# The second MLP product as seven half-size block products instead of eight, with the sums on VectorE

## The chip, the cores and the metric

The kernel runs on one core of a Trainium2 chip. The metric is the device time of one execution in microseconds (us). A core has TensorE (PE, matrix products, with its weight loads listed apart as PEld), VectorE (DVE), ScalarE (ACT), GpSimd (POOL) and SyncE (SP), which mainly issues DMAs. Each engine runs its own queue of instructions in order; semaphores tie the queues together. Products land in PSUM, and DVE or ACT must take them out of it ("drain" it) before a bank can be used again.

## The reference

Attention with a local window of 96 keys and 8 global keys, then a mixing step and an MLP with layer norm, cut to what matters:

```python
def _attn_ref(q, k, v, n_global, n_local):        # (4, 8, 768, 64)
    scores = scale * np.matmul(q, k.transpose(0, 1, 3, 2))
    ...
    scores = np.where(keep, scores + bias, -1e9)
    a = np.exp(scores - max); a = a / sum(a)
    return np.matmul(a, v)
def _moe_ref(x, w_ch1, w_ch2):                     # x (4, 768, 512)
    mixed = np.real(np.fft.fft(np.fft.fft(x, axis=1), axis=2))
    u = x + mixed
    un = (u - mean(u)) / np.sqrt(var(u) + 1e-6)
    ch = np.maximum(un @ w_ch1, 0.0) @ w_ch2       # 512 -> 2048 -> 512
    return u + ch
```

The change concerns the last product, `relu(...) @ w_ch2`, and the sum behind it.

## The kernel before

**Tiling.** The four batches have 768 rows each. The MLP works in chunks of 256 rows, three to a batch, so 12 chunks, c = 0 to 11. A chunk has two row tiles t of 128.

**Per batch.** Attention: `trans` turns q and k of a head pair into qkT (pt, L449), `score` makes the scores (sc, L493), ACT takes their exponentials (er, L516), DVE multiplies them with a mask (ex, L531), and `av` makes the output (pav, L612 and L623), which DVE normalizes into x (L643). `bounce` writes x to DRAM and reads it back in another order as xr. `fold_s` and `fold_d` (L686 to L755, called f1 to f4, g1 and g2 here) are sums and differences on DVE that shrink the Fourier step; `y_unit` (py, L775 and L778) makes its first product, `mirror` reverses parts on POOL, `u_unit` (pu, L856) makes the second, and DVE adds xr to give u (L875). A scaled copy un is transposed by `nt_unit` (ptu, L920) to unT.

**Per chunk.** `ph_unit`, eight per chunk, makes two blocks of 128 of the 2048 hidden columns (ph, L948, 8 matmuls of 256 columns each); ACT (L954) or DVE (L955) takes the relu into hT, [128, 16 blocks, 256 rows] fp16. `pg_unit`, two row tiles by four parts, multiplies hT with w2 (pg, L971, 16 matmuls of 512 columns for a row tile, in one PSUM bank); then one DVE instruction (L982) adds pg, scaled by 1/std, to u, into an output buffer ob, which SP writes to DRAM (L987).

**Order.** A planner in the kernel (`Plan`) writes every queue out when the program is built. It holds four streams of TensorE work, in order of preference: MIX (mixing step), ATT (attention), PH (first product) and PG (second product). From MIX and ATT it may pick among the next ten units, from PH and PG only the first. It gives every DVE, ACT, POOL and SP step an assumed duration, keeps a clock for each engine, and picks the unit that it thinks can start first. So second products fill TensorE where nothing else is ready. The order is then fixed: an engine waits at the head of its queue.

**Buffers.** NBUF gives the number of rotating buffers of each name: hT 3, qs (staging of q and k) 3, u 4, x 1, xr 1, ob 2. PSUM has two banks for pg. In batch 0 hT's buffers also take q and k of three head pairs, and the fourth goes through qs. Weights are loaded by POOL (`wload`, L1057 and L1060), w1 early and w2 in four parts after the last v cast of batch 1.

Of the kernel before, what the change touches and what calls it, by code (L numbers as in the profile page):

```python
# [14 lines left out]
P = 128  # L15
# [144 lines left out]
def dve(n):  # L160
    return 0.15 + n / 960.0


def dve2(n):
    return 0.16 + n / 1920.0
# [7 lines left out]
def kernel(  # L173
# [82 lines left out]
    def bank(tag, name, dtype=FP32):  # L256
# [4 lines left out]
        if "late" not in early:  # L261
# [4 lines left out]

    NBUF = {"hT": 3, "vs": 2, "qk": 2, "qs": 3, "qkT": 4, "er": 2, "eg": 1, "x": 1, "xr": 1, "zy": 1, "eA": 1,
            "ww": 1, "rev0": 1, "u": 4, "un": 2, "unT": 2, "ob": 2}

# [17 lines left out]
    w1 = kon.tile([P, ND, 4 * Dm], FP16, tag="w1", name="w1")  # L287
    w2 = kon.tile([P, NJ, Dm], FP16, tag="w2", name="w2")
    mhalf = kon.tile([P, 2], FP32, tag="mhalf", name="mhalf")
# [16 lines left out]
    def load(b, hp, which):  # L306
# [11 lines left out]
        elif which == "v":  # L318
# [6 lines left out]
            pl.later([("SP", 0.9, run)], free(vtag, vi) + gate, 0.0, [("ld", "v", n)], lat=1.6, dma=2.45)  # L325
        elif b == 0 and hp < 3:
            cell = {}

            def run(cell=cell):
                cell[0] = buf("hT", hp, [P, 2, NS, 2 * Dh], FP32, 2)  # L330
                for w, src in enumerate((q, k)):
                    qk_dma(cell[0][:, w], src, b, h0)
            pl.later([("SP", 0.9, run)], free("hT", hp), 0.0, [("ld", "qk", n, w) for w in range(2)], lat=1.6, dma=2.4)
            for w in range(2):
                cast_qk(b, hp, w, lambda w=w, cell=cell: cell[0][:, w], ("hT", hp))
        else:
            for w, src in enumerate((q, k)):
                cell = {}
                i = 2 * (n - 3) + w

                def run(cell=cell, src=src, i=i):
                    cell[0] = buf("qs", i, [P, NS, 2 * Dh], FP32, 1)
                    qk_dma(cell[0], src, b, h0)
                pl.later([("SP", 0.45, run)], free("qs", i) + gate, 0.0, [("ld", "qk", n, w)], lat=1.6, dma=1.2)
                cast_qk(b, hp, w, lambda cell=cell: cell[0], ("qs", i))
# [251 lines left out]
    def av(b, part, jp):  # L597
# [8 lines left out]
        def run(start, ring):  # L606
# [31 lines left out]
            def norm():  # L638
                if b not in X:
                    X[b] = buf("x", b, [P, NS, Dm], FP16, 4 if b else 5)  # L640
                rc = wk.tile([P, 2, nh, 1], FP32, tag="rc", name=f"rc_{b}_{first}_{jp}", bufs=2)
                V.reciprocal(rc, pv[:, :, :, 64:65])
                VT(X[b][:, 2 * jp:2 * jp + 2, first * Dh:(first + nh) * Dh].rearrange("p j (h d) -> p j h d", d=Dh),  # L643
                   pv[:, :, :, 0:Dh], rc.to_broadcast([P, 2, nh, Dh]), op=ALU.mult)
            pl.later([("DVE", 0.18 + dve(128 * nh), norm)], free("x", b), e, [("x", b, hp, jp) for hp in part], CD(b),
                     ring=ring, rank=RA(b))
# [5 lines left out]
    def bounce(b):  # L652

        on, eng = ("ACT", nc.scalar) if b else ("SP", nc.sync)
        for half in range(2):
            def wr(half=half):
# [4 lines left out]
                for t in range(2):  # L661
                    eng.dma_start(rows[t], X[b][64 * t:64 * t + 64, :, c])
            pl.later([(on, 1.2, wr)], [("x", b, hp, jp) for hp in (2 * half, 2 * half + 1) for jp in range(NP)] + [("xw", b, 0)][:half], 0.0,
                     [("xw", b, half)], [("free", "x", b)], lat=1.6, dma=2.5)

        def rd():
            XR[b] = buf("xr", b, [P, NS, Dm], FP16, 3)
            rows = XD[b].rearrange("(m r) d -> m r d", r=6)
            eng.dma_start(XR[b], rows)
        pl.later([(on, 0.5, rd)], [("xw", b, 0), ("xw", b, 1)] + free("xr", b), 0.0, [("xr", b)], lat=1.6, dma=4.0)  # L670

    def fold_s(b):
# [3 lines left out]
        for n, (c0, cw) in enumerate(parts):  # L676
# [25 lines left out]
            def f4(c0=c0, cw=cw, cell=cell):  # L702
# [6 lines left out]
                     + (free("zy", 2 * b) if n == 0 else []), 0.0,  # L709
                     [("f1", b, n)], [("free", "x", b)] * (2 if len(hps) == HP else 1))  # L710
            pl.later([("DVE", 2 * dve2(2 * cw), f2)], [("f1", b, n)] + free("ww", IW(b, n)), 0.0, [("f2", b, n)])
# [133 lines left out]
    def u_unit(b, pr):  # L845
# [4 lines left out]
        def run(start, ring):  # L850
# [20 lines left out]
            def add():  # L871
                u = UT[c] = buf("u", HP + c, [P, 2, Dm], FP32, 2)
                sm = MV[c] = wk.tile([P, 2, 4], FP32, tag="sm", name=f"sm_{c}", bufs=6)
                for a, rr in enumerate((r0, r1)):
# [5 lines left out]
            pl.later([("DVE", 2 * dve(512) + 0.15, add)], [("xr", b)] + free("u", HP + c), e, [("u", c)],  # L880
                     [("free", "xr", b)] + CD(b), ring=ring)
            cell = {}
# [55 lines left out]
    def ph_unit(c, jp):  # L938
        needs = [("unT", c), ("w1", jp // 2)] + (free("hT", 3 + c) if jp == 0 else []) + [("CD",)]

        def run(start, ring):
            if jp == 0:
                HT[c] = buf("hT", 3 + c, [P, NJ, CH], FP16, 2)
            ph = bank("ph", f"ph_{c}_{jp}")
# [12 lines left out]
        PH.append((needs, ("ph",), run))  # L957

    GP = {}

    def pg_unit(c, t, part):
        b, pr = divmod(c, NP)
        rs = PAIRS[pr][t]
        needs = [("h", c, 2 * part), ("h", c, 2 * part + 1), ("w2", part)]

        def run(start, ring):
            if part == 0:
                GP[0] = bank("pg", f"pg_{c}_{t}")
            pg = GP[0]
            for jb in range(4 * part, 4 * part + 4):  # L970
                nc.tensor.matmul(pg, HT[c][:, jb, t * P:(t + 1) * P], w2[:, jb, :],  # L971
                                 start=(jb == 0), stop=(jb == NJ - 1))
            e = pl.pe(mm_us(512, 4), start)
            if part < 3:
                return
            pl.used(("free", "hT", 3 + c), e)
            i = 2 * c + t
            cell = {}

            def add():  # L980
                cell[0] = buf("ob", i, [P, Dm], FP32, 1)
                V.scalar_tensor_tensor(cell[0], pg, MV[c][:, t, 3:4], UT[c][:, t, :],  # L982
                                       op0=ALU.mult, op1=ALU.add)
            pl.later([("DVE", dve(512), add)], [("rstd", c)] + free("ob", i), e, [("ob", i)], [("free", "u", HP + c)], ring="pg", rank=0)

            def st():
                nc.sync.dma_start(out[b].rearrange("(m r) d -> m r d", r=6)[:, rs, :], cell[0])  # L987
            pl.later([("SP", 0.45, st)], [("ob", i)], 0.0, [], [("free", "ob", i)], lat=1.6, dma=0.7)
        PG.append((needs, ("pg",) if part == 0 else None, run))

# [4 lines left out]
    with tc.manual_schedule():  # L995
# [58 lines left out]
        def wload(i):  # L1054
# [4 lines left out]
            else:  # L1059
                nc.gpsimd.dma_start(w2[:, 4 * a:4 * a + 4, :],  # L1060
                                    moe_w_ch2[a * 512:(a + 1) * 512, :].rearrange("(c p) f -> p c f", p=P))
        for i in range(8):
            needs = [("ld", "qk", 3, 1)] if i == 0 else [("v", 1, HP - 1)] if i == 4 else [("wl", i - 1)]
            pl.later([("POOL", 0.85, lambda i=i: wload(i))], needs, 0.0,
                     [("w1" if i < 4 else "w2", i % 4)], lat=2.0, dma=2.6, rank=1 if i < 4 else 2,
                     then=lambda t, i=i: pl.tok.__setitem__(("wl", i), pl.t["POOL"]))
        for b in range(B):
            if b:
# [52 lines left out]
        for c in range(NP * B):  # L1121
            for jp in range(NJ // 2):
                ph_unit(c, jp)
            for t in range(2):
                for part in range(4):
                    pg_unit(c, t, part)
        pl.run([(MIX, True), (ATT, True), (PH, False), (PG, False)])
# [35 lines left out]
```

The softmax here doesn't subtract the row's maximum and nothing guards it: scores larger than these inputs give would overflow.

## Time and profile before

| what | value |
|---|---|
| timed runs | 290.87, 291.68 and 292.29 us; median 291.68 |
| profiled execution | span 288.0 us from first to last instruction; its own total is not listed apart |
| median less span | 3.7 us |
| PE, PEld busy | 256.0 (89%), 172.7 (60%) |
| DVE, ACT, POOL busy | 183.3 (64%), 142.5 (49%), 59.2 (21%) |
| first product ph, 768 matmuls | 94.0 us busy |
| second product pg, 384 matmuls | 91.1 us busy |
| drains of pg, 24 on DVE | 18.0 us busy |
| moved by DMA | 37.04 MB, 129 GB/s mean |

Busy time of an engine is the union of its instructions; the mean duration of a group can be longer than the distance between two of its instructions, since they overlap. The page cuts the span into 40 slices of 7.2 us and gives the busy share of each engine in tenths. In the group lists each row has the source line, engine, operation, output and inputs, count, then busy time and mean duration, then the idle time in front of it and what ended it.

### The profile page before, as it was taken

What the parts mean: (1) busy time and instruction counts of PE and PEld (TensorE: products, weight loads), DVE (VectorE), ACT (ScalarE), POOL (GpSimd) and SP (SyncE); (2) the same over time, 40 slices, a digit from 0 to 9 for tenths busy, and PEclk for the clock granted to TensorE, in tenths of its full rate; (3) what the DMA queues carried; (4) which work ended last, traced back from release to release, by engine and by line L of the source; (5) the groups of instructions that cost most, each with busy time, mean ns of one, the idle gap of its engine ahead of it and who ended that gap; (6) DMA issues with size and microseconds to landing.
All of it is one profiled execution on the core that took longest, in us unless ns stands there. A gap on an engine that the chain in (4) does not pass through costs nothing.

```text
span 288.0 us, 5961 instructions
## 1 busy us (share of the span) xinstructions
PE 256.0 (89%) x2436; PEld 172.7 (60%) x2436; DVE 183.3 (64%) x380; ACT 142.5 (49%) x224; POOL 59.2 (21%) x124
## 2 busy tenths in 40 slices
PE   1788338799886999989999999999999999999994
PEld 1335226687654646677688466875775767777441
DVE  3516997877744997887679968675897582211121
ACT  2577803888744315567754235778142255544100
POOL 1373006237211111641101113301000411100000
PEclk9999859999997999999999999999999999999999
DMA  7999979799999999913302711100144010010111
GB/s 215 289 293 184 191 237 179 162 216 180 186 220 158 241 253 278 225 52 105 109 2 68 245 73 39 40 0 2 45 103 148 36 73 2 36 39 0 73 75 73
DMA packets 62378, 37.04 MB, mean 129 GB/s; under 512 B 20368, under 2 KB 58512, under 8 KB 62352
## 3 DMA queue, kind: packets, MB, share of 16 engines
q1 hardware_dynamic: 52896, 27.76, 40.0%
q0 software_dynamic: 4224, 4.19, 9.3%
q10 hardware_dynamic: 5232, 4.72, 5.7%
q8 instruction: 19, 0.31, 0.5%
q14 instruction: 7, 0.06, 0.1%
HBM read 31.42 MB, written 9.44 MB: 142 GB/s over the span
## 4 chain that ended last, share of the span: by engine, by line
PE 76%; DMA 9%; DVE 7%; SPq 3%; ACT 3%; issue 1%; DVEq 0%; ACTq 0%
PE pg L971 28%; PE ph L948 26%; DMA qs<-in_k_dram 6%; PE sc L493 3%; PE pav L623 3%; PE pu L856 3%; PE pt L449 3%; SPq L349 3%; PE py L775 2%; DMA qs<-in_q_dram 2%; PE ptu L920 2%; PE py L778 2%; DVE u L875 1%; PE pav L612 1%; DVE x L643 1%
## 5 line engine op out<-in xcount | busy, mean ns | idle before, releaser
L948 PE MATMUL ph<-unT,w 128*128 128x256 f16 x768 | 94.0, 273 | 2.4 <-DVE u L875 2.1
L971 PE MATMUL pg<-w,hT 128*128 128x512 f16 x384 | 91.1, 382 | 0.0
L948 PEld LDWEIGHTS <-w 128*128 128x128 f16 x768 | 71.8, 98 | 18.3 <-issue 7.8
L971 PEld LDWEIGHTS <-hT 128*128 128x128 f16 x384 | 36.4, 98 | 37.1 <-issue 2.0
L954 ACT ACTIVATE hT<-ph 128x512 f16<-128x512 f32 x56 | 33.4, 597 | 39.1 <-PE ph L948 39.0
L982 DVE SCALAR_TENSOR_TENSOR ob<-pg,sm,u 128x512 f32<-128x512 f32 x24 | 18.0, 750 | 41.7 <-PE pg L971 37.5
L516 ACT ACTIVATE er<-sc 128x992 f16<-128x992 f32 (+2 forms) x36 | 32.8, 923 | 19.1 <-PE sc L493 16.9
L955 DVE TENSOR_SCALAR hT<-ph 128x512 f16<-128x512 f32 x40 | 27.5, 689 | 22.3 <-PE ph L948 22.2
L531 DVE TENSOR_TENSOR ex<-er,mk 128x992 f16<-128x992 f16 (+2 forms) x36 | 23.3, 653 | 5.0 <-ACT er L516 4.9
L360 ACT ACTIVATE qk<-qs 128x768 f16<-128x768 f32 x21 | 17.3, 839 | 18.2 <-DMA qs<-in_k_dram 7.3
L824 POOL COPY ww<-zy 128x512 f16<-128x512 f16 x16 | 10.0, 654 | 55.4 <-PE py L775 33.8
L791 ACT ACTIVATE zy<-py 128x512 f16<-128x512 f32 (+1 forms) x12 | 9.6, 810 | 21.6 <-PE py L778 13.3
L623 PE MATMUL pav<-v,ex 128*128 128x65 f16 x352 | 16.7, 196 | 3.8 <-ACT er L516 3.0
L455 DVE COPY qkT<-pt 128x1536 f16<-128x1536 f16 x15 | 14.3, 951 | 8.8 <-PE pt L449 8.8
L775 PE MATMUL py<-t,ww 128*128 128x256 f16 x48 | 11.9, 303 | 8.9 <-DVE ww L740 8.9
L623 PEld LDWEIGHTS <-ex 128*128 128x128 f16 x352 | 15.6, 99 | 6.6 <-issue 4.7
L493 PE MATMUL sc<-qkT 64*128 64x256 f16 (+1 forms) x192 | 17.6, 265 | 1.0 <-DVE qkT L455 1.0
L643 DVE TENSOR_TENSOR x<-pav,rc 128x512 f16<-128x512 f32 (+1 forms) x27 | 17.1, 632 | 0.9
L875 DVE SCALAR_TENSOR_TENSOR u<-pu,xr 128x512 f32<-128x512 f32 x24 | 15.6, 687 | 2.3 <-PE pu L856 2.0
L420 POOL CAST v<-vs 128x768 f16<-128x768 f32 x12 | 10.6, 885 | 27.2 <-DMA vs<-in_v_dram 27.0
L464 POOL COPY kG<-qkT 64x8 f16<-64x8 f16 x32 | 7.8, 244 | 38.6 <-DVE qkT L455 37.7
L449 PE MATMUL pt<-ident,qk 128*128 128x128 f16 x192 | 14.0, 225 | 1.9 <-ACT er L516 0.9
(93 smaller groups left out, 286.3 us busy)
## 6 DMA issues: line engine op xcount, KB each, us to landing
out_dram<-ob SPq DMA_DIRECT2D x24, 256.0 KB, 2.0
qs<-in_q_dram SPq DMA_DIRECT2D x13, 384.0 KB, 5.4
qs<-in_k_dram SPq DMA_DIRECT2D x13, 384.0 KB, 6.5
vs<-in_v_dram SPq DMA_DIRECT2D x24, 192.0 KB, 6.7
w<-in_moe_w_ch_dram POOLq DMA_DIRECT2D x8, 512.0 KB, 10.0
xd<-x ACTq DMA_DIRECT2D x12, 192.0 KB, 3.8
xr<-xd ACTq DMA_DIRECT2D x3, 768.0 KB, 4.3
u<-in_v_dram SPq DMA_DIRECT2D x4, 384.0 KB, 6.3
```

The source lines that it names most:

```text
L449: nc.tensor.transpose(o[:, j % 2], src[:, w, j].rearrange("p h d -> p (h d)"), idn)
L493: nc.tensor.matmul(pa[:, s, c0:c0 + cw], TT[n][lo:lo + 64, 1, i * P:(i + 1) * P], TT[n][lo:lo + 64, 0, i * P:i * P + cw], start=(b > 0), s ...
L516: A(mine(), cut(pa), AF.Exp, 0.0, 0.125)
L531: VT(o, mine(), m, op=ALU.mult)
L623: nc.tensor.matmul(po[:, jj, hh * 65:(hh + 1) * 65], lhsT, v16[b % 2][:, i, h, 0:65], start=(jp == 0 and a == 0), stop=(a == len(ops) - 1) ...
L643: VT(X[b][:, 2 * jp:2 * jp + 2, first * Dh:(first + nh) * Dh].rearrange("p j (h d) -> p j h d", d=Dh), pv[:, :, :, 0:Dh], rc.to_broadcast( ...
L875: V.scalar_tensor_tensor(u[:, a].rearrange("p (n r) -> p n r", r=4), pu[:, a].rearrange("p (r n) -> p n r", r=4), 1.0, XR[b][:, rr].rearra ...
L948: nc.tensor.matmul(ph[:, a * CH:(a + 1) * CH], w1[:, d, jb * P:(jb + 1) * P], UNT[c][:, d, :], start=(d == 0), stop=(d == ND - 1))
L954: pl.later([("ACT", act(512), lambda: A(dst, ph, AF.Relu)), ("DVE", dve(512), lambda: V.tensor_scalar_max(dst, ph, 0.0))], [], e, [("h", c ...
L955: ("DVE", dve(512), lambda: V.tensor_scalar_max(dst, ph, 0.0))],
L971: nc.tensor.matmul(pg, HT[c][:, jb, t * P:(t + 1) * P], w2[:, jb, :], start=(jb == 0), stop=(jb == NJ - 1))
L982: V.scalar_tensor_tensor(cell[0], pg, MV[c][:, t, 3:4], UT[c][:, t, :], op0=ALU.mult, op1=ALU.add)
```

## The change

hT's 16 hidden blocks are the inner dimension of the product. Split it in halves: h is then a 2x2 block matrix (row tile t by half of the hidden columns), w2 one too (half of its rows by half of its 512 columns). Eight block products of 8 matmuls of 256 columns would give the output; Winograd's form of Strassen's method needs seven and some sums. After the change:

- `w2_sums`: eight fp16 DVE sums of 1024 elements, once, give the weight blocks w2t (three of them) and one in place.
- `s_sums`: four DVE sums of 1024 elements a chunk: S1 and S2 and S4 in buffers sx, S3 in place in hT.
- `pg_units`: seven products in five units (p1; p45; p6; p32; p7) in two PSUM banks, A and D. Bank A is drained after p1, after p6 and after p7, bank D after p45 and after p32. Each drain scales by 1/std and accumulates into u in place; p7's goes to both column halves. Products that several outputs share are added on their drained copies or stay in the bank for the next product.
- The output is written from u; ob goes. hT has 2 buffers instead of 3, qs 2 instead of 3; x and xr share one. Batch 0's third and fourth q and k are staged in the space that w2 takes afterwards, and w2's parts are loaded in the order 0, 2, 1, 3.

```diff
-    NBUF = {"hT": 3, "vs": 2, "qk": 2, "qs": 3, "qkT": 4, "er": 2, "eg": 1, "x": 1, "xr": 1, "zy": 1, "eA": 1,
-            "ww": 1, "rev0": 1, "u": 4, "un": 2, "unT": 2, "ob": 2}
+    NBUF = {"hT": 2, "vs": 2, "qk": 2, "qs": 2, "qkT": 4, "er": 2, "eg": 1, "x": 1, "zy": 1, "eA": 1,
+            "ww": 1, "rev0": 1, "u": 4, "un": 2, "unT": 2, "w2": 1, "sx": 4}
...
-            XR[b] = buf("xr", b, [P, NS, Dm], FP16, 3)
+            XR[b] = buf("x", 2 * b + 1, [P, NS, Dm], FP16, 3)
...
+    def w2_sums(i):
+        def run():
...
+            VT(w2t[:, 1, k0, :], b22, b12, op=ALU.subtract)
+            VT(b12, b12, b11, op=ALU.subtract)
+            VT(w2t[:, 0, k0, :], b22, b12, op=ALU.subtract)
+            VT(w2t[:, 2, k0, :], b21, w2t[:, 0, k0, :], op=ALU.subtract)
+        pl.later([("DVE", 4 * dve2(1024), run)], [("w2", i), ("w2", 2 + i)], 0.0, [("w2t", i)], rank=1)
...
+        def s1():
+            VT(new(0), block(1, 0), block(1, 1), op=ALU.add)
+        def s3():
+            VT(block(1, 0), block(0, 0), block(1, 0), op=ALU.subtract)
+        def s2():
+            VT(new(1), SX[c, 0], block(0, 0), op=ALU.subtract)
+        def s4():
+            VT(new(2), block(0, 1), SX[c, 1], op=ALU.subtract)
...
-            for jb in range(4 * part, 4 * part + 4):
-                nc.tensor.matmul(pg, HT[c][:, jb, t * P:(t + 1) * P], w2[:, jb, :],
-                                 start=(jb == 0), stop=(jb == NJ - 1))
...
+        def prod(o, lhs, rhs, first, last=True):
+            for j in range(NK):
+                nc.tensor.matmul(o, lhs(j), rhs(j), start=(first and j == 0), stop=(j == NK - 1), skip_group_check=True)
...
+        def p1(start, ring):
+            A_ = GP[c, "A"] = bank("pg", f"pgA_{c}")
+            prod(A_[:, 0:HC], a(0, 0), bw(0, 0), True)
...
+            pl.later([("DVE", dve(HC), lambda: stt(u(0)[:, 0:HC], A_[:, 0:HC], 0, u(0)[:, 0:HC]))],
...
+        def p45(start, ring):
+            D_ = GP[c, "D"] = bank("pg", f"pgD_{c}")
+            prod(D_[:, 0:HC], a(1, 1), tw(2), True)
+            prod(D_[:, HC:Dm], sx(0), bw(0, 1), True)
...
+        def p6(start, ring):
+            prod(A_[:, 0:HC], sx(1), tw(0), False)
...
+        def p32(start, ring):
+            prod(D_[:, HC:Dm], sx(2), bw(1, 1), False)
+            prod(D_[:, 0:HC], a(0, 1), bw(1, 0), True)
...
+        def p7(start, ring):
+            prod(A_[:, 0:HC], a(1, 0), tw(1), False)
...
+                stt(o, A_[:, 0:HC].unsqueeze(1).to_broadcast([P, 2, HC]), 1, o)
...
+        PG.append((h0 + ws, ("pg",), p1))
+        PG.append((h1 + [("s", c, 1)], ("pg",), p45))
+        PG.append(([("s", c, 2), ("ra", c, 0)], None, p6))
+        PG.append(([("s", c, 4), ("rd", c, 0)], None, p32))
+        PG.append(([("s", c, 3), ("ra", c, 1)], None, p7))
```

## The prediction

> **What bounds the kernel now.** I read the page's parts 1 and 2 first, then the busy time by stretches, the groups by line, and the timeline where attention of one batch ends. Engine rows, then the fortieths of the span:
>
> ```profile
> PE 256.0 (89%) x2436; PEld 172.7 (60%) x2436; DVE 183.3 (64%) x380; ACT 142.5 (49%) x224; POOL 59.2 (21%) x124
> ...
> PE   1788338799886999989999999999999999999994
> ...
> DVE  3516997877744997887679968675897582211121
> ...
> PEclk9999859999997999999999999999999999999999
> DMA  7999979799999999913302711100144010010111
> ```
>
> TensorE is nearly full from the fourteenth slice on; before that it starves while the DMA engines are at 9. VectorE (DVE) is the second engine, and its slack lies in the last quarter, not in the middle. The stretches (length, then PE, PEld, DVE, ACT, POOL busy, clock, DMA share, GB/s):
>
> ```profile
> 60.00:89.00 29.00, 25.22 (x256) 18.19 (x254) 18.32 (x28) 20.44 (x32) 8.92 (x18) 1.00 1.16 198
> 89.00:113.00 24.00, 23.27 (x201) 13.57 (x199) 20.20 (x38) 6.96 (x9) 4.01 (x8) 0.93 1.04 242
> 113.00:169.00 56.00, 54.85 (x559) 38.57 (x558) 46.44 (x86) 31.48 (x50) 13.23 (x24) 1.00 0.45 117
> 169.00:221.00 52.00, 52.00 (x533) 37.41 (x531) 40.29 (x80) 27.86 (x46) 7.91 (x19) 1.00 0.17 56
> 236.00:288.00 52.00, 48.04 (x323) 31.01 (x321) 9.93 (x18) 16.58 (x31) 1.77 (x4) 0.99 0.12 46
> ```
>
> From 89 to 221 DVE is 77 to 84% busy already. The groups concerned (by form), and the fold stage of batch 2 in the timeline:
>
> ```profile
> L948 PE MATMUL ph<-unT,w 128*128 128x256 f16 x768 | 94.0, 273 | 2.4 <-DVE u L875 2.1 <-ACT unT L928 0.2
> L971 PE MATMUL pg<-w,hT 128*128 128x512 f16 x384 | 91.1, 382 | 0.0
> L971 PEld LDWEIGHTS <-hT 128*128 128x128 f16 x384 | 36.4, 98 | 37.1 <-issue 2.0
> L982 DVE SCALAR_TENSOR_TENSOR ob<-pg,sm,u 128x512 f32<-128x512 f32 x24 | 18.0, 750 | 41.7 <-PE pg L971 37.5 <-DMA out_dram<-ob 2.9 <-issue 1.2
> ...
> L692 DVE TENSOR_TENSOR ww<-eA 128x1024 f16<-128x1024 f16 x3 | 2.1, 693 | 0.2
> ```
>
> ```profile
> 156.92 7.07 PE L971 MATMUL pg<-w,hT 128*128 128x512 f16 x32
> 159.84 0.74 DVE L982 SCALAR_TENSOR_TENSOR ob<-pg,sm,u 128x512 f32<-128x512 f32 x1
> 165.98 0.27 PE L775 MATMUL py<-t,ww 128*128 128x256 f16 x1
> 166.85 2.75 PE L971 MATMUL pg<-w,hT 128*128 128x512 f16 x12
> ```
>
> This is what matters: the second product is TensorE's filler. While DVE folds (about 155 to 167) and while y becomes the next unT (py at 165.98, first ph at 180.52 in the chain), pg runs, and 16 of its matmuls ask DVE for one drain. L971 never waited (0.0).
>
> **What the Trainium skill says.** "VectorE: DVE Perf Modes", section "The perf-mode tier table (the rule you actually need)": a two-tensor 16-bit op within SBUF goes at most at 2x, one with a PSUM operand at 1x. The trace agrees: 1024 fp16 elements take 693 ns, 512 fp32 out of PSUM 750. "GPSIMD Engine Reference", section "1. Specifications": GpSimd's SBUF interfaces are shared with DVE instructions that have two SBUF inputs. The trace fits: the 1536-element subtraction L687 took 1.58 us beside a POOL cast at 155.9, about 0.95 otherwise. "TensorE: Matmul & The Clock Gate", section "Why this matters for your kernels": idle gaps over some 3 us cost clock. Here, after the pause at 85.6 to 88.6, the clock of 88 to 92 was 0.61.
>
> **The change, part by part.** Durations are of the profiled execution, whose span is 288.0. Its own total isn't listed apart; I take the median run's 291.68 and call the 3.7 us beyond the span constant.
>
> *TensorE, removed.* 80 pg matmuls run in 17.28 us in the chain, 0.216 each; 16 ph matmuls of 256 columns in 1.75, 0.109 each. Before 384 x 0.216 = 82.9; after 12 chunks x 7 products x 8 = 672 x 0.109 = 73.5. **Gain 9.4**; the work left is 256.0 - 9.4 = 246.6. The 288 further weight loads cost nothing: one takes 98 ns, under the 109 of its matmul, as in L948.
>
> *DVE, added.* Back to back the 1024-element fp16 ops start 0.61 apart (99.80, 100.41, 101.01): 48 sums on h are 29.3 and 8 on the weights 4.9. A chunk's drains become three of 512 and two of 256 instead of two of 512. A 512 drain holds DVE 0.65 (159.84 to 160.50). A 256 one isn't shown: its bounds are 0.20 (pitch of a 256-element fp16 op) and 0.65; I take 0.38, since in L643 256 elements less save 0.27. So 12 x (3 x 0.65 + 2 x 0.38) = 32.5 against 15.6, +16.9. **Sum +51**, DVE about 234. That fits the span; where it falls doesn't.
>
> *Early, 60 to 89.* hT falls from three buffers to two, so in TensorE's queue 16 ph units stand ahead of the first product where 24 stood, and the third chunk waits for all seven products of the first. The products need all of w2 and the weight sums. w2 is still issued on POOL's queue behind the fourth v cast (66.2 in the trace) and landed 10 to 14.6 us after issue, so by about 83; eight sums end near 88. Out of 60 to 89 go 8 ph units (7.0), eight pg matmuls (1.7) and the scores of the last head pair (1.0); one product (0.9) comes in. TensorE is busy 25.2 - 8.8 = 16.4 of 28: idle 11.6, 3.8 before. About 2 us of low clock follow (0.61 above). qs falls from three buffers to two: q and k loads on SP's queue wait for a cast sooner and the v loads behind them as well; v is reordered ahead of q there, so I charge nothing. The w2 loads, the fp16 cast and this wait are hidden by the same starvation.
>
> *Fold stages.* I walked both queues for batch 1, zero at the last av matmul. DVE: norm to 1.1, f1 to f3 with a drain and a relu to 6.4, f4 and the second chunk's drains to 10.2, g1 to 12.1, its last drains 13.4. TensorE ends that chunk at 11.8, but the third chunk's first product reuses the bank, and starts at 13.5: stall 1.7. Then S2, a drain, S3 and g2 (to 17.5) stand on DVE ahead of the drain of the D bank and S4 (19.1); P3 needs both while TensorE stopped at 17.0: stall 2.2. py, though ready at 12.1, is queued behind P3 and starts at 20.9. From there to the first ph (about 32.6) only P7 (0.9) is left as filler, where before 36 matmuls (7.8 us) lay: idle some 3. In all **7** for batch 1; batch 2 by the same walk **8** (1.0 + 1.5 + 2.6, then 3); batch 3, whose order keeps two products after py, **6**.
>
> *Elsewhere.* Between folds DVE has about 30 us of work against 37 of TensorE: 1 us each for the first product behind the last drain, 2 in all. At the end, the last chunk's D drain stands behind S2, S3, S4 on DVE: stall 1.5; drain and output are the 4.0 of before.
>
> *At nothing:* out written from u instead of ob (the same 24 writes on SP; u comes free a landing, 2 us, later, but has four buffers and is next needed after the fold); x and xr sharing one buffer (the read waits for f1, done while the xd writes land, 3.8); batch 0's fourth q and k staged in w2's space (w2 is not loaded before 66).
>
> *Sum.* Work 246.6; idle before 60: 60 - 37.6 = 22.4, kept; 11.6 + 2 early; 7 + 8 + 6 folds; 2; 5.5 end: 311.1. Matmul ends, 0.16 us each, are in the 256 as busy and overlap some 20 stalls: minus 3. Span 308.1, **time 311.8**.
>
> **The rivals.**
> - *Faster: TensorE stays covered.* For it: L971 waited 0.0, and DVE has a third of the span free. Then 9.4 is gained and about 3 lost early: 291.7 - 9.4 + 3 = 285. It decides once all added idle stays under 9.4, that is w2 summed by 80 and each fold's stalls under 2 us. Against it: the folds' DVE queue leaves no room, and the filler is finished before the latency it covered. 0.05; a draw at 291 another 0.05.
> - *Half the stalls.* Short drains at the lower bound and ACT taking relus let DVE run ahead: folds 10 instead of 21, early 3 less: 298 to 300. 0.22.
> - *DVE the outright bound.* The sums run at one element a cycle, for strides or for POOL's sharing. By L643's slope 256 elements cost 0.27, so 1024 would cost 0.5 more: 56 x 0.5 = 28 on DVE, of which I put half on the path: 326. For it: the 1.58 us. Against: L531's masked 960-element ops, strided too, take 685 ns. 0.12.
> - My forecast 0.56.
>
> That the change computes other than it says I find no room for: 672 matmuls stand in the queue.
>
> **How the numbers follow.** The likeliest gives 311.8. The range, 297 to 325, takes the half-stall case, the unknown drains, and most of the outright bound; it leaves out the draw and the gain. About 0.5% is what a measurement of this kernel tells from no change: faster 0.05, same 0.05, slower 0.90.
>
> **What would show it.** The product line with 672 matmuls near 73 to 82 us busy; its waits now on DVE, 15 us or more; DVE 225 to 245 busy; TensorE's slices near 76 to 88 at about half; three dips after the first 100 us, each before the first ph of a batch; relus of ACT idling longer. I am wrong if TensorE stays at 9 throughout, if w2t's sums end before 80, or if the sums average over 1 us.

## The result, and the profile after

The changed kernel takes **314.37 us** (median of four runs, 312.40 to 316.37), the kernel before 291.27 beside it: ratio **1.081, 95% interval 1.073 to 1.090**; the medians are 23.1 us apart. The profiled execution has a span of 311.0 us, 23.0 more than the 288.0 before. Some executions of one and the same kernel ran at a lower granted clock and took longer; the ratios leave them out, and the profiles of e5_load and e1_qs3 are of such executions.

First the page, engine rows and fortieths of the span (a slice is 7.8 us now):

```profile
PE 255.5 (82%) x2724; PEld 204.1 (66%) x2724; DVE 232.3 (75%) x468; ACT 143.7 (46%) x228; POOL 59.6 (19%) x124
...
PE   2798077993199987779999976789999987899994
...
DVE  3438979899648997588779996677788998762553
...
PEclk9799679997569998999999997999999999999998
```

TensorE's busy time has not fallen (255.5 against 256.0), VectorE's rose by 49.0. TensorE's row of nines has three dips after the first 100 us (slices 15 to 18, 24 to 27 and 33 to 35), each before a batch's first `ph`; in the row before, only slice 18 read under 9 there, with an 8. The clock row has new digits under 9 as well.

The stretches are cut at the same events as the forecast's stages: first `ph` of batch 0, then for each batch its last `av` matmul and its first `ph`. Columns: length, then PE, PEld, DVE, ACT, POOL busy, granted clock, DMA share, GB/s.

```profile
52.40:102.10 49.70, 38.03 (x413) 29.64 (x410) 38.46 (x62) 25.14 (x40) 18.56 (x29) 0.83 1.09 200
102.10:136.70 34.60, 27.47 (x273) 23.00 (x272) 27.93 (x57) 12.33 (x16) 5.87 (x13) 0.95 0.63 162
136.70:171.50 34.80, 34.80 (x409) 27.71 (x406) 28.51 (x50) 22.76 (x40) 5.07 (x11) 1.00 0.23 67
171.50:205.00 33.50, 25.82 (x258) 21.46 (x255) 27.59 (x56) 11.03 (x14) 4.97 (x12) 0.95 0.31 97
205.00:239.90 34.90, 34.90 (x409) 27.82 (x407) 28.14 (x49) 20.89 (x38) 4.08 (x10) 1.00 0.07 23
239.90:265.90 26.00, 21.67 (x218) 18.47 (x216) 24.27 (x51) 6.88 (x10) 3.07 (x7) 1.00 0.29 94
265.90:311.00 45.10, 40.70 (x376) 35.96 (x375) 22.44 (x37) 15.65 (x32) 2.64 (x6) 0.98 0.10 36
```

Length less PE busy is TensorE's idle time. In the two attention stages (third and fifth line) it is nil; before it was 0.9 and 0. In the fold stages (second, fourth, sixth) it is 7.1, 7.7 and 4.3 us. Before, the same three stages were these, with 0.25, 0 and 0 us idle:

```profile
96.60:121.20 24.60, 24.35 (x179) 13.79 (x176) 21.77 (x39) 9.57 (x12) 7.71 (x15) 1.00 1.09 247
...
154.00:180.40 26.40, 26.40 (x213) 16.29 (x212) 22.75 (x44) 11.11 (x16) 6.76 (x14) 1.00 0.32 108
...
209.80:235.70 25.90, 25.90 (x204) 17.07 (x203) 19.90 (x40) 8.41 (x14) 3.77 (x9) 1.00 0.26 84
```

The fold stages of batches 1 and 2 have become 10.0 and 7.1 us longer, the early stretch (first line of after) 5.6, the attention stages 2.0 and 5.5, since they take over products (64 each, where they had 4 and 16 of twice the width); for the same reason the tail is 7.2 shorter (45.1 against 52.3). That is the 23.0.

The groups by line and form show the new product line, L1019, whose 672 matmuls are in six rows, and what DVE got:

```profile
L1019 PE MATMUL pgD<-w,sx 128*128 128x256 f16 x192 | 26.7, 285 | 5.3 <-DVE sx L1005 5.3
L1037 DVE SCALAR_TENSOR_TENSOR u<-pgD,sm,u 128x512 f32<-128x512 f32 x24 | 18.0, 748 | 17.9 <-PE pgD L1019 17.9
L1019 PE MATMUL pgD<-w,hT 128*128 128x256 f16 x96 | 14.2, 297 | 0.0
L1019 PE MATMUL pgD<-w2t,hT 128*128 128x256 f16 x96 | 13.3, 285 | 0.3 <-DVE u L1037 0.3
L1019 PE MATMUL pgA<-w,hT 128*128 128x256 f16 x96 | 13.3, 285 | 1.9 <-DVE u L1037 1.8
L1019 PE MATMUL pgA<-w2t,sx 128*128 128x256 f16 x96 | 12.5, 273 | 1.6 <-DVE sx L1002 1.6
L1019 PE MATMUL pgA<-w2t,hT 128*128 128x256 f16 x96 | 12.4, 273 | 0.0
L1037 DVE SCALAR_TENSOR_TENSOR u<-pgA,sm,u 128x256 f32<-128x256 f32 x24 | 11.5, 481 | 8.4 <-PE pgA L1019 8.4
...
L1005 DVE TENSOR_TENSOR sx<-hT,sx 128x1024 f16<-128x1024 f16 x12 | 8.2, 682 | 0.0
```

The six rows add up to 92.4 us, where 384 matmuls of twice the width took 91.1. The line that never waited now waits 9.1 us, for drains (L1037), S2 (L1002) and S4 (L1005).

The timeline of batch 2's fold stage, PE and DVE, shows one such place. Columns: start, length, then the instruction, and in brackets the idle time ahead of it with its releaser.

```profile
182.34 0.95 DVE L744 TENSOR_TENSOR eA<-zy 128x1536 f16<-128x1536 f16 x1
...
183.80 0.55 DVE L747 TENSOR_TENSOR ww<-eA 128x768 f16<-128x768 f16 x1
184.27 0.48 DVE L1037 SCALAR_TENSOR_TENSOR u<-pgA,sm,u 128x256 f32<-128x256 f32 x1
184.67 0.74 DVE L1037 SCALAR_TENSOR_TENSOR u<-pgD,sm,u 128x512 f32<-128x512 f32 x1
185.32 0.68 DVE L1002 TENSOR_TENSOR sx<-sx,hT 128x1024 f16<-128x1024 f16 x1
...
186.06 1.05 PE L1019 MATMUL pgA<-w2t,sx 128*128 128x256 f16 x8 [1.57 <-DVE sx L1002]
...
188.33 0.48 DVE L1037 SCALAR_TENSOR_TENSOR u<-pgA,sm,u 128x256 f32<-128x256 f32 x1
188.72 0.68 DVE L1005 TENSOR_TENSOR sx<-hT,sx 128x1024 f16<-128x1024 f16 x1
...
189.46 1.53 PE L1019 MATMUL pgD<-w,sx 128*128 128x256 f16 x8 [2.35 <-DVE sx L1005]
190.79 1.91 PE L1019 MATMUL pgD<-w,hT 128*128 128x256 f16 x8
...
192.49 0.42 PE L781 MATMUL py<-t,ww 128*128 128x256 f16 x1
```

DVE is full, and folds, drains and sums take turns on it. TensorE waits 1.57 us for S2 and 2.35 for S4. `py`, whose input ww (L747) was ready at 184.35, is queued behind the products and starts at 192.49 (the products aren't all that holds it: see the folds below). The same windows by the microsecond show a second cost, in the granted clock (last column but two):

```profile
188.00:189.00 1.00, 0.00 (x0) 0.00 (x0) 1.00 (x5) 0.00 (x0) 0.00 (x0) 1.00 0.00 0
189.00:190.00 1.00, 0.54 (x5) 0.47 (x6) 1.00 (x2) 0.00 (x0) 0.00 (x0) 0.94 0.00 0
190.00:191.00 1.00, 1.00 (x6) 0.70 (x5) 1.00 (x2) 0.00 (x0) 0.37 (x2) 0.50 0.09 16
191.00:192.00 1.00, 1.00 (x6) 0.75 (x5) 0.14 (x1) 0.00 (x0) 0.37 (x2) 0.50 0.00 0
192.00:193.00 1.00, 1.00 (x7) 0.69 (x6) 0.26 (x1) 0.00 (x0) 0.00 (x0) 0.50 0.00 0
193.00:194.00 1.00, 1.00 (x10) 0.84 (x9) 0.49 (x1) 0.04 (x1) 0.00 (x0) 0.86 0.00 0
```

After the two pauses the matmuls run at half clock for over 3 us; a group of eight takes 1.91 us instead of 1.04.

### The profile page after: what moved, and what is told of

Same layout as the page of the kernel before. It is cut to its first block, busy times and chain, and to the rows that moved or that the text cites. A ratio compares the mean times of both kernels' runs of the same rounds, so it can differ in the third digit from the quotient of the medians.

```text
span 311.0 us, 6644 instructions
## 1 busy us (share of the span) xinstructions
PE 255.5 (82%) x2724; PEld 204.1 (66%) x2724; DVE 232.3 (75%) x468; ACT 143.7 (46%) x228; POOL 59.6 (19%) x124
## 4 chain that ended last, share of the span: by engine, by line
PE 60%; DVE 24%; DMA 8%; ACT 3%; issue 2%; POOL 2%; SPq 1%; POOLq 0%; DVEq 0%
PE ph L954 25%; PE pgD L1019 11%; PE pgA L1019 7%; DMA qs<-in_k_dram 6%; DVE u L1037 4%; DVE u L881 4%; PE sc L499 3%; PE pt L455 3%; PE pav L629 3%; DMA u<-in_v_dram 2%; PE py L781 2%; DVE x L649 2%; ACT ex L525 2%; PE py L784 2%; DVE eA L744 1%
## 5 line engine op out<-in xcount | busy, mean ns | idle before, releaser
L960 ACT ACTIVATE hT<-ph 128x512 f16<-128x512 f32 x58 | 34.5, 596 | 55.1 <-PE ph L954 55.1
L1019 PEld LDWEIGHTS <-hT 128*128 128x128 f16 x384 | 39.0, 102 | 8.8 <-issue 3.0
L1019 PEld LDWEIGHTS <-sx 128*128 128x128 f16 x288 | 28.1, 100 | 12.6 <-DVE sx L1005 6.1
L1037 DVE SCALAR_TENSOR_TENSOR u<-pgD,sm,u 128x512 f32<-128x512 f32 x24 | 18.0, 748 | 17.9 <-PE pgD L1019 17.9
L1019 PE MATMUL pgD<-w,sx 128*128 128x256 f16 x192 | 26.7, 285 | 5.3 <-DVE sx L1005 5.3
L961 DVE TENSOR_SCALAR hT<-ph 128x512 f16<-128x512 f32 x38 | 26.1, 689 | 6.5 <-PE ph L954 6.3
L797 ACT ACTIVATE zy<-py 128x1024 f16<-128x1024 f32 (+1 forms) x12 | 10.2, 880 | 44.8 <-PE py L784 32.3
L1037 DVE SCALAR_TENSOR_TENSOR u<-pgA,sm,u 128x256 f32<-128x256 f32 (+1 forms) x36 | 20.3, 570 | 13.4 <-PE pgA L1019 13.1
L537 DVE TENSOR_TENSOR ex<-er,mk 128x992 f16<-128x992 f16 (+2 forms) x36 | 22.4, 636 | 1.2 <-ACT er L522 1.1
L455 PE MATMUL pt<-ident,qk 128*128 128x128 f16 x192 | 15.6, 241 | 9.2 <-ACT qk L366 9.0
L461 DVE COPY qkT<-pt 128x1536 f16<-128x1536 f16 x15 | 14.2, 955 | 9.1 <-PE pt L455 8.9
L455 PEld LDWEIGHTS <-qk 128*128 128x128 f16 x192 | 13.1, 108 | 10.8 <-ACT qk L366 9.5
L881 DVE SCALAR_TENSOR_TENSOR u<-pu,x 128x512 f32<-128x512 f32 x24 | 15.6, 688 | 3.8 <-PE pu L862 3.8
## 6 DMA issues: line engine op xcount, KB each, us to landing
out_dram<-u SPq DMA_DIRECT2D x24, 256.0 KB, 2.0
```

The costliest lines, as they stand in the source:

```text
L455: nc.tensor.transpose(o[:, j % 2], src[:, w, j].rearrange("p h d -> p (h d)"), idn)
L537: VT(o, mine(), m, op=ALU.mult)
L881: V.scalar_tensor_tensor(u[:, a].rearrange("p (n r) -> p n r", r=4), pu[:, a].rearrange("p (r n) -> p n r", r=4), 1.0, XR[b][:, rr].rearra ...
L960: pl.later([("ACT", act(512), lambda: A(dst, ph, AF.Relu)), ("DVE", dve(512), lambda: V.tensor_scalar_max(dst, ph, 0.0))], [], e, [("h", c ...
L961: ("DVE", dve(512), lambda: V.tensor_scalar_max(dst, ph, 0.0))],
L1019: nc.tensor.matmul(o, lhs(j), rhs(j), start=(first and j == 0), stop=(j == NK - 1), skip_group_check=True)
```

## The experiments

Each theory's expectation is quoted as it stood before the run. Ratios are to the kernel before, run on the same chip with it (medians 291.85, 290.28 and 290.00 us in the three groups of runs), with their 95% intervals.

| label | what it is | us | ratio | interval |
|---|---|---|---|---|
| e1_buf | after's buffers, old product | 296.19 | 1.016 | 1.009 to 1.024 |
| e1_qs3 | the same, qs 3 | 294.54 | 1.015 | 1.007 to 1.022 |
| e1_hT3 | the same, hT 3 | 302.56 | 1.044 | 1.038 to 1.050 |
| e5_load | e1_buf and 48 sums that nobody reads | 305.68 | 1.049 | 1.041 to 1.057 |
| e8_bare | after, no sums at all, drains of one column | 298.17 | 1.029 | 1.023 to 1.036 |
| e4_neither | the same, with the weight sums | 298.82 | 1.025 | 1.017 to 1.034 |
| e2_noS | after without the sums on h | 303.00 | 1.038 | 1.032 to 1.045 |
| e3_short | after with drains of one column | 305.08 | 1.045 | 1.039 to 1.052 |
| e9_gate | after, a filler moved | 316.22 | 1.088 | 1.082 to 1.095 |
| e7_qs3 | after with qs 3, sx 3 | 318.69 | 1.095 | 1.089 to 1.101 |
| e6_tail9_11 | before, new form for chunks 9 to 11 | 288.41 | 0.996 | 0.993 to 0.999 |
| e6_tail910 | before, new form for chunks 9 and 10 | 290.28 | 1.004 | 0.998 to 1.010 |

**e1_buf: the buffers without the products.** The changed kernel with the old 16 matmuls of 512 columns and their one drain for each row tile; w2_sums and s_sums go.

```diff
-            s_sums(c)
-            pg_units(c)
+            for t in range(2):
+                for part in range(4):
+                    pg_unit(c, t, part)
...
-        for i in range(2):
-            w2_sums(i)
```

> The changed kernel's buffers and staging (hT 2, qs 2, x and xr shared, output summed in u, w2 in the staging space, w2 parts in the order 0, 2, 1, 3) with the old product: 16 matmuls of 512 columns and one drain per row tile, no sums. Theory A (the time lost lies in the fold stages, where products wait on VectorE, plus an early starvation that the fewer buffers make): only the early part stays, 297 to 301 us, TensorE's dip near 80 us kept and the fold stages full again. Theory B (all of it is VectorE's work, the fewer buffers are hidden): 291 to 293.

Measured: 296.19 us, between the two. hT 2, qs 2, the staging in w2's space and the shared x, with the order that the planner writes for them, cost some 5 us without any seven-product form. The loss isn't where theory A put it:

```profile
53.50:99.00 45.50, 40.56 (x417) 28.41 (x415) 27.50 (x46) 25.63 (x41) 14.93 (x27) 0.96 1.19 217
99.00:128.10 29.10, 24.01 (x203) 14.98 (x200) 23.81 (x48) 11.28 (x16) 7.25 (x14) 1.00 0.74 195
```

The early stretch leaves TensorE 4.9 us idle, hardly more than the 4.5 of the kernel before, while the fold stages of batches 1 and 2 leave it 5.1 (second line) and 1.1. So TensorE has less filler in the folds even with the old product, and the early starvation of the changed kernel doesn't come from the buffers alone.

**e2_noS, e3_short, e4_neither: the two halves of DVE's new work.** One leaves out the sums on h and lets the products read unsummed blocks; one lets every drain touch one column, which leaves out the rest of the output; one does both. Products, units, waits for drains and the order stay.

```diff
-            VT(new(1), SX[c, 0], block(0, 0), op=ALU.subtract)
+            new(1)
...
-            return lambda j: SX[c, i][:, j, :]
+            return a(*((1, 0), (1, 1), (0, 1))[i])
```

```diff
-            pl.later([("DVE", dve(Dm), lambda: stt(u(1), D_, 1, u(1)))],
+            pl.later([("DVE", dve(Dm), lambda: stt(u(1)[:, 0:1], D_[:, 0:1], 1, u(1)[:, 0:1]))],
```

> The changed kernel with the 48 sums on h (S1 to S4) left out, the products taking plain blocks of hT instead; the queues of all engines keep their order otherwise. The outputs are not the reference's. VectorE loses 29 us of work. Theory A (sums and drains both stand between products in the fold stages): about half of the folds' 21 us comes back, 302 to 307. Theory C (the five drains per chunk alone set the pace, the sums fill VectorE's free time): 312 to 315.

> The changed kernel with each of the 60 drains cut to one column (as many instructions and waits, each about 0.1 to 0.2 us instead of 0.48 or 0.75), sums kept, order kept. Most of the output is left unadded. Theory A: VectorE loses about 27 us of work, some 4 us of it in each fold stage: 302 to 307. Theory D (the handshakes between TensorE and VectorE cost, not the length of what VectorE does): 312 to 315.

> Both of the last two: no sums on h, drains of one column; the products stay 672 of 256 columns, order kept. The output is not the reference's. Theory A: the folds' stalls go, the 9.4 us of TensorE work stay saved and the early starvation stays: 292 to 298. Theory D (handshakes and the order of the queues cost by themselves): 303 or more.

Measured: 303.00, 305.08 and 298.82. Without sums 11.4 us go, with short drains 9.3, with both 15.5. The last is just above its band, and less than the two together: either one alone makes most of the room, so what counts is how long DVE's queue is, not which of the two kinds stands in it. It counts in the fold stages: the three together take 81.6 us in e4_neither and 94.1 in the changed kernel, 12.5 of the 15.3 by which the spans differ. The rival of 303 or more, in which both leave the bound in place, falls.

**e8_bare: no sums at all.** As e4_neither, and w2_sums emptied; the products read plain blocks of w2.

```diff
-            VT(w2t[:, 1, k0, :], b22, b12, op=ALU.subtract)
...
+            pass
...
-            return lambda j: w2t[:, i, j, :]
+            return bw(*((0, 0), (0, 1), (1, 1))[i])
```

> The changed kernel with neither sums on h, nor full drains, nor now the sums on the weights: it leaves out all of the added VectorE work, so the products read unsummed blocks and the output is another. What is left of the change: seven products, two banks, five units, and the smaller buffers. With neither sums on h nor full drains it took 298.8. Theory A (VectorE's sums on the weights, 4.9 us of work on the path between w2's arrival and the first product, hardly count, since the first product waits for the cast of the last q and k in front of it on TensorE's queue): 297.5 to 299. Rival W (the weight sums set the start of the second product, as the prediction had it): 294 to 296.

Measured: 298.17; that the weight sums count for anything can't be told from e4_neither. Its page and its fold stages:

```profile
PE 249.1 (84%) x2724; PEld 201.6 (68%) x2724; DVE 172.5 (58%) x412; ACT 143.8 (49%) x228; POOL 57.8 (20%) x124
```

```profile
101.00:130.50 29.50, 25.45 (x273) 22.24 (x271) 21.47 (x53) 12.46 (x16) 6.24 (x13) 1.00 0.74 189
...
165.40:193.30 27.90, 23.74 (x257) 20.71 (x256) 21.21 (x52) 11.05 (x14) 4.97 (x12) 1.00 0.37 116
...
228.20:252.30 24.10, 21.10 (x217) 18.69 (x216) 18.28 (x47) 6.87 (x10) 3.07 (x7) 1.00 0.31 102
```

The order is that of the changed kernel. DVE is given back more than the change took: it is busy 172.5 us against 183.3 in the kernel before, since drains of one column leave out work that the old product had too. So what this run gains is the most that the added work can be charged with. The span falls from 311.0 to 296.1; of the 14.9 us, 8.5 are idle time (55.5 to 47.0) and 6.4 are busy time of the same 2724 matmuls (255.5 to 249.1). Batch 2's fold shows the second part: 257 matmuls in 23.74 us at a clock of 1.00, against 258 in 25.82 at 0.95. And even so the form isn't faster than e1_buf's old product. TensorE works 8.3 us less (249.1 against 257.4), but idles 47.0 us instead of 36.1: 11.2 in the three fold stages and 11.2 in the early stretch, where e1_buf has 6.2 and 4.9.

**e5_load: load without dependence.** e1_buf with four sums a chunk of 1024 elements each, written to a scrap tile. No product waits for them, though a buffer of hT comes free only after them; the order's planner is not told their time.

```diff
+            pl.later([("DVE", 0.0, run)], hs + [("xs", c, n - 1)][:n], 0.0, [("xs", c, n)], [("free", "hT", 2 + c)], rank=1)
...
+            extra(c)
```

> The buffers of the changed kernel with the old product (as e1_buf), plus 48 fp16 sums of 1024 elements on VectorE, four per chunk as soon as its h is there, written to a scratch tile that nobody reads; nothing waits for them, the planner gives them no time, the results are the reference's. VectorE gets 29 us more. Theory A (a product that depends on VectorE several times per chunk is what stalls TensorE, since pg with one drain per 16 matmuls still fills): 0 to 5 us above e1_buf. Theory E (VectorE's load alone delays folds and so everything): 10 us or more above e1_buf.

Measured: 305.68, 9.5 more than e1_buf. A's 0 to 5 falls, and E's 10 or more is nearly reached. It isn't necessary that a product waits for a sum: 48 sums, some 33 us of DVE time among folds and drains, cost 9.5 even where nobody reads the result.

**e9_gate and e7_qs3: two repairs that failed.** The first holds the third chunk's products back until batch b+1's first y is under way, so that they can cover the latency behind `py`. The second gives q and k their third staging buffer, paid for with one sx.

```diff
-        PG.append((h0 + ws, ("pg",), p1))
+        gate = [("y", b + 1, 2, 0)] if pr == 2 and b + 1 < B else []
+        PG.append((h0 + ws + gate, ("pg",), p1))
```

```diff
-    NBUF = {"hT": 2, "vs": 2, "qk": 2, "qs": 2, "qkT": 4, "er": 2, "eg": 1, "x": 1, "zy": 1, "eA": 1,
-            "ww": 1, "rev0": 1, "u": 4, "un": 2, "unT": 2, "w2": 1, "sx": 4}
+    NBUF = {"hT": 2, "vs": 2, "qk": 2, "qs": 3, "qkT": 4, "er": 2, "eg": 1, "x": 1, "zy": 1, "eA": 1,
+            "ww": 1, "rev0": 1, "u": 4, "un": 2, "unT": 2, "w2": 1, "sx": 3}
```

> The changed kernel with one need more: the third chunk of batches 0, 1 and 2 starts its seven products only when the next batch's first y is there, so that they lie between y, u and the next unT instead of inside the fold. Same work, results the reference's. Theory A (the filler was used up inside the fold, where VectorE held it, and lacked behind py): 5 to 10 us faster than the changed kernel, 304 to 309. Theory F (VectorE's chain through the fold sets the time, wherever the products lie): 312 to 316.

> The changed kernel with three buffers for qs instead of two and three for sx instead of four (which pays for it), results the reference's. In the changed kernel's trace TensorE waits 9.0 us for the cast of the last q and k of batch 1 while the weight sums end 0.8 us before its first product. Theory G (two qs buffers make that wait): the wait shrinks by 5 us or more and the time falls by 3 to 7. Theory H (w2 and its sums would hold the first product anyway, and the DMA engines are full): within 2 us of the changed kernel.

Measured: 316.22 and 318.69. Neither gains; the first lies at the edge of F's band, the second is 4.3 us slower than the changed kernel, more than H allowed, though their intervals just overlap. In e9_gate `py` of batch 1 starts 18.4 us after the last `av` matmul (22.0 in the changed kernel), and from there to the first `ph` TensorE is busy all of 13.8 us: the products do cover the latency. But the first `ph` still comes after 32.2 (34.6 in the changed kernel), since the wait has moved ahead of `py`, where TensorE now stands for 6.4 us until DVE has copied qkT (L461). In e7_qs3 the early wait of `pt` for the cast of q and k (9.0 us) is gone, and the waits of TensorE, in all, times and longest, name another:

```profile
PE sc L499 <- ACT er L522: 8.9, 2, 8.5
...
PE pgD L1019 <- DVE sx L1005: 4.7, 2, 2.4
```

The 8.5 us end at 86.27, no earlier than the wait that is gone (85.05). Since sx went from 4 to 3 with it, this run doesn't show what the third qs does by itself.

**e1_qs3 and e1_hT3: which buffer?** e1_buf with one of the two numbers set back.

```diff
-    NBUF = {"hT": 2, "vs": 2, "qk": 2, "qs": 2, "qkT": 4, "er": 2, "eg": 1, "x": 1, "zy": 1, "eA": 1,
+    NBUF = {"hT": 3, "vs": 2, "qk": 2, "qs": 2, "qkT": 4, "er": 2, "eg": 1, "x": 1, "zy": 1, "eA": 1,
```

> The old second product with the changed kernel's buffers (296.2 us), but with three hT buffers again; qs stays at two. If the 4.6 us that those buffers cost come from hT (fewer first products stand ahead as filler while w2 is loaded), 291.5 to 293. If they come from qs (q and k loads wait for a cast), 295.5 to 297.

> The old second product with the changed kernel's buffers (296.2 us), but with three qs buffers again; hT stays at two. If the 4.6 us come from hT: 295.5 to 297. If they come from qs: 291.5 to 293. If both are near 296, each alone is enough to cost it; if both are near 293, they share it.

Measured: 302.56 and 294.54. The third qs makes no difference that can be told, and the third hT made it worse, which nobody expected: batch 1's fold stage is 32.9 us long with 9.7 idle at a clock of 0.74 there. Each number makes the planner write another order, so these runs don't divide the 5 us between the buffers; that stays open.

**e6_tail9_11 and e6_tail910: the form where DVE has room.** The kernel before, with its buffers; only the chunks after the last fold stage use the seven products. The sums on the weights come after the last u, in tiles that are free by then.

```diff
+    FAST = (9, 10, 11)
...
-                HT[c] = buf("hT", 3 + c, [P, NJ, CH], FP16, 2)
+                HT[c] = buf("hT", 3 + c, [P, NJ, CH], FP16, 1 if c in FAST else 2)
...
+            if c in FAST:
+                s_sums(c)
+                pg_units(c)
+                continue
```

> The kernel before, with its buffers, and the seven-product form for chunks 9, 10 and 11 alone, where VectorE was 10 us busy of 52; its weight sums start once the last u is there, and w2t and sx lie in tiles that attention no longer needs. Results the reference's. Theory A (products save 0.8 us a chunk where VectorE has room; the last chunk's drains cost 1.5 at the end): 0 to 2 us faster than before, 289 to 291. Theory D (handshakes cost everywhere): 1 to 4 us slower than before.

> The kernel before with the seven-product form for chunks 9 and 10 alone; chunk 11, the last, keeps the old sixteen matmuls of 512 columns for each row tile. Against the form for 9 to 11 it gives up one chunk's gain of TensorE work (16 x 0.216 x 2 less 56 x 0.109 = 0.8 us), and gets rid of the stall at the very end, where the last chunk's products wait for the sums and drains of that chunk (4.4 us of TensorE idle at the end of the changed kernel, 4.0 before). Theory A (the end costs the form about 0.5 to 1): 287.5 to 288.5, equal to 288.4 or slightly under. Rival (the gain is per chunk, the end free): 289.0 to 289.5.

Measured: 288.41 and 290.28. The first is a little faster than the kernel before, 0.4% with an interval of 0.1 to 0.7%, the best version of all; the second is a draw, above the bands of both its theories, so the idea that the last chunk costs the form more than it gains finds no support. From first `ph` to the last product e6_tail9_11 takes 46.8 us where the kernel before took 48.3. Its two last stages:

```profile
208.40:234.40 26.00, 26.00 (x207) 17.19 (x204) 19.92 (x40) 8.41 (x14) 3.78 (x9) 1.00 0.26 84
234.40:285.20 50.80, 46.48 (x399) 38.27 (x396) 26.90 (x46) 17.26 (x32) 2.38 (x5) 1.00 0.13 48
```

The fold stage keeps its full cover (26.00 of 26.00 busy). In the tail DVE goes from 10 to 27 us of 51, and TensorE idles 4.3 us where it was 4.0.

## Why the prediction was right, and where it was not

The forecast was 311.8 us and the mechanism in the fold stages was the one that the runs show: DVE has no room there, products wait for it, `py` comes late, and too little filler is left behind it. TensorE's idle time by stage (us), with the forecast's own stages on the same rows:

| stage | before | forecast | after | e8_bare |
|---|---|---|---|---|
| start, and early (to last av of batch 1) | 26.9 | 34.0 | 32.0 | 32.4 |
| fold of batch 1 | 0.3 | 7 | 7.1 | 4.1 |
| fold of batch 2 | 0 | 8 | 7.7 | 4.2 |
| fold of batch 3 | 0 | 6 | 4.3 | 3.0 |
| attention of batches 2 and 3 | 0.9 | 2 | 0 | 0 |
| tail and end | 4.0 | 5.5 | 4.4 | 3.4 |
| sum | 32.0 | 62.5 | 55.5 | 47.0 |

(The forecast cut at 60 and 89 us, not at the first `ph` and the last `av`; its 22.4 and 11.6 are taken together.)

- **DVE, +51.** Measured +49.0. The drain of 256 columns, unknown before, was taken at 0.38 us; the next DVE instruction starts 0.40 later (184.27, 184.67). The rival that the sums run at one element a cycle falls: 682 to 726 ns each.
- **Folds.** The walk put the first `ph` 32.6 us after batch 1's last `av` matmul, and the trace has 34.6. For batch 1 it named two stalls, 1.7 and 2.2, and the trace has 1.36 and 2.08; for batch 2 three, 1.0, 1.5 and 2.6, and the trace has 0.1, 1.57 and 2.35. Behind `py` it expected some 3 us without filler; the trace has 3.7, 3.7 and 3.0. Batch 3 was put too high. e8_bare parts the two: the stalls all but go, and the idle time behind `py` stays as it was, so of the 19.1 us DVE's work is worth 7.9, and 11.2 remain. The traces show that there is less filler, 14.4, 13.7 and 12.0 us of products in the three stages against 18.6, 17.6 and 16.2 before; how much of that is the form, the buffers or the order was not tested apart.
- **When `py` is ready.** The walk called `py` ready at 12.1 and took only the products for what holds it. `py` also needs a PSUM bank of the two that the transposes `pt` use before it, and their copies (L461) stand behind S4 on DVE, from 189.32 in batch 2. In e8_bare it is such a copy that releases `py`:

```profile
181.18 0.27 PE L781 MATMUL py<-t,ww 128*128 128x256 f16 x1 [0.48 <-DVE qkT L461]
```

  So in the changed kernel, too, `py` could hardly have started before about 190.2, the end of the first copy; of its delay only the last 2.3 us, by this estimate, are those of the products ahead of it.
- **Early, right in size, but not in the wait that it named.** From 60 to 89 the trace has 11.7 us of idle time, the forecast 11.6 (part of that is luck: its sum takes 28 us for a stretch of 29). It let the first product wait for all of w2 and its sums, and charged qs nothing. The last sum is done at 84.91 and the first product starts at 85.66, but TensorE stood before that at the transposes of the last q and k, waiting for their cast:

```profile
83.11 0.82 PE L455 MATMUL pt<-ident,qk 128*128 128x128 f16 x6 [7.92 <-ACT qk L366]
...
84.22 0.69 DVE L982 TENSOR_TENSOR w2t<-w,w2t 128x1024 f16<-128x1024 f16 x1
...
85.05 0.82 PE L455 MATMUL pt<-ident,qk 128*128 128x128 f16 x6 [1.12 <-ACT qk L366]
...
85.66 1.91 PE L1019 MATMUL pgA<-w,hT 128*128 128x256 f16 x8
```

  In e8_bare, with no weight sums, the first product starts at 85.49, so it isn't the sums that hold it. Nor do two qs buffers explain the loss: e1_buf has them too, and its old products cover the time until the same transposes, each part of a product as soon as its quarter of w2 is there:

```profile
78.00 2.40 PE L980 MATMUL pg<-w,hT 128*128 128x512 f16 x6 [2.31 <-DMA w<-in_moe_w_ch_dram]
...
82.50 2.75 PE L980 MATMUL pg<-w,hT 128*128 128x512 f16 x12 [1.25 <-DMA w<-in_moe_w_ch_dram]
85.09 1.05 PE L454 MATMUL pt<-ident,qk 128*128 128x128 f16 x12
```

  In the changed kernel a first product needs all of w2, whose last part DVE waits for until 82.04, and it stands behind those transposes in the queue. So of the forecast's early step, the need for all of w2 fits the runs, and the sums as what holds the product don't. No run tests the need for all of w2 alone.
- **TensorE's work, mis-sized by 9.** The sum took 246.6 us of work, and set 2 of low clock against 3 of overlapping ends; the page has 255.5. Two terms. The smaller is the number of groups: the forecast's pitch makes 672 matmuls 73.5 us, and e8_bare's product line takes 84.0, so 10.5 are left for the ends of groups, where no next matmul overlaps the last one, and for some low clock between 85 and 89; before it was 91.1 less 82.9, 8.2. "TensorE: Matmul & The Clock Gate", section "Single matmul latency", gives a warm matmul (398 + N)/2.4 ns, so 166 ns of it do not depend on its width; the trace agrees, a group of eight takes 1.04 us, 8 x 0.109 and 0.17 more. The larger is the 6.4 us between e8_bare and the changed kernel, most of it the clock: busy time times what the clock lacks of 1.00, summed over every microsecond of the span, is an estimate of what low clock costs, and gives 10.3 us in the changed kernel, 4.8 in e8_bare and 3.5 before. The forecast's 2 of low clock, all early, came true (3.7 against 1.6 before, from 52 to 101); the 3.4 in the folds of batches 1 and 2 it did not have.
- That error of +9.9 (255.5 against 245.6) and 7.0 less idle time made the span 2.9 longer than forecast. The total is near partly because two misses have opposite signs, and that is luck. The 3.7 us that it set between span and median is 3.4 here: 1.7 by which the profiled execution (312.74) is longer than its span, and 1.6 by which the median run is longer than that one.
- **Signs.** DVE at 225 to 245 us busy and three dips came; so did the idle relus of ACT (55.1 us before L960, 39.1 before). The product line was to take 73 to 82 us and took 92.4, its waits on DVE were to be 15 us or more and are 9.1, and near 76 to 88 TensorE was to be about half busy, where slice 11 (77.8 to 85.5) reads 1.
- **Rivals.** The faster one needed each fold's stalls under 2 us: they were 4 to 8. Half the stalls (298 to 300) is where e8_bare lies, with less DVE work than the kernel before.

So of the 8% some 15 to 16 us are DVE's added work, at most (after less e8_bare, e4_neither): that part is shown with the order of the queues kept. By the ratios some 5 are the buffers (e1_buf) and 2 to 4 the form itself (e8_bare and e4_neither less e1_buf, whose intervals overlap); these two are not clean, since each comes with an order of its own, and e1_hT3 shows that one buffer more, with its order, can cost 6 to 8 us. The saving of multiplications is real, 8.3 us of PE time between e1_buf and e8_bare, and is spent there on idle time; in the changed kernel itself PE's busy time fell by only 0.5.

## What to carry to other kernels

A product that fills another engine's gaps is worth what it covers; price work that is added to the second engine in the stage where that engine is already full, not over the span, where a third of it looked free. Here such a trade of multiplications for sums paid only in a stretch where the summing engine had room for all of it, the tail, and even there 1.5 us. When a walk of the queues gives the right total, still check each wait's releaser afterwards: one of these was another than named.

## What the runs showed of the hardware that was not expected

The clock fell after pauses that were each short. "TensorE: Matmul & The Clock Gate", section "Why this matters for your kernels", warns of gaps of over some 3 us. Here gaps of 1.57 and 2.35 us, with one group of 1.05 between them, were followed by a clock of 0.50 from 190 to 193; in batch 1's fold gaps of 1.36 and 2.08 us, with 3.7 us of matmuls between them, were followed by a clock of 0.50 from 122 to 125. In e8_bare's fold of batch 2, with 4.2 us of idle time in pieces of 1.1 us at most, it stayed at 1.00. In the first two folds the added stalls came with 4.1 us of added busy time (27.47 and 25.82 against 25.45 and 23.74), 3.4 of it the clock by the estimate above. In the third fold, with gaps of 0.42 and 0.82 us at the products, the clock stayed at 1.00 and 0.6 us were added all the same (21.67 against 21.10). So here a stall had to be priced with what it does to the clock, too. That the gaps bring the clock down is read from what followed what; no run moves the gaps alone.
